# Routed attention and a hard-swish feed-forward block on one core: larger transposition groups, a new order in the prologue, and a fall-through at the close

## The chip, the cores and the metric

The kernel runs on one core of a Trainium2 chip. The metric is the device time of the whole launch in microseconds (us), taken as the median of several runs. The kernel before takes 1071.25 us (3 runs, 1070.79 to 1073.04). Beside the timed runs there is one profiled execution, whose first to last instruction span 1069.7 us.

## The reference, cut to what matters

Attention in which a query sees only the keys of its own cluster, then a feed-forward block. Batch 4, 8 heads, 768 positions, head dimension 64, 16 clusters; the block has 3072 tokens, width 512 and inner width 2048.

```python
q_assign = np.argmax(np.einsum('bhsd,hcd->bhsc', q_n, c_n), axis=-1)   # nearest centroid
k_assign = np.argmax(np.einsum('bhsd,hcd->bhsc', k_n, c_n), axis=-1)
mask = q_assign[:, :, :, None] == k_assign[:, :, None, :]
scores = scale * np.matmul(q, k.transpose(0, 1, 3, 2))
scores = np.where(mask, scores, -1000000000.0)
attn = softmax(scores)                      # with 1e-9 in the denominator
x = (attn @ v), heads side by side          # (4*768, 512)
h = x @ w_in
out = (h * np.clip(h + 3.0, 0.0, 6.0) / 6.0) @ w_out
```

The weights arrive as 64-bit floats and are decoded on the chip into 32-bit ones.

## The kernel before

Two heads are worked on together (a pair; there are 16), each with 768 positions as 6 chunks of 128. For each pair the queries and keys are transposed (`turn`), scored against the centroids (`cluster_scores`), turned into one-hot rows of the nearest cluster (`route`), and those rows are transposed (`route_turn`). For keys the one-hot rows are inverted and scaled by a large negative number, so that a second matmul into the same scores (`xm`) adds zero where the clusters agree and a large negative number elsewhere. Then come the exponential, the product with the values and a division.

A transposition on TensorE writes to PSUM, and ScalarE copies the result to SBUF. The transpositions and other small results share scratch banks of PSUM: two banks (`psum_m`) in the first half, one (`psum_t`) later.

```python
psum_t = pool("psum_t", 1, space=PSUM)
psum_m = pool("psum_m", 2, space=PSUM)

def scratch(shape, name):
    if st["early"]:
        return psum_m.tile(shape, F32, name=name, tag="m")
    return psum_t.tile(shape, F32, name=name, tag="t")

def turn(g, part):                     # four parts of NHC = 3 chunks
    ...
    pt = scratch([P, NHC, P], "pqk")
    for i in range(NHC):
        j = part * NHC + i
        nc.tensor.transpose(out=pt[:, i], in_=qk[:, j // NCH, j % NCH], identity=ident)
    dst = xf[:, part * NHC : (part + 1) * NHC]
    nc.scalar.copy(out=dst, in_=pt)
    ...

def route_turn(g, part):               # three parts of 4 chunks
    ...
    po = scratch([P, 4, P], "po")
    for i in range(4):
        j = part * 4 + i
        nc.tensor.matmul(
            po[:, i], lhsT=one_hot[:, j], rhs=(ident_q if j < NCH else ident_k),
            start=True, stop=True,
        )
    nc.scalar.copy(out=xm[:, part * 4 : part * 4 + 4], in_=po)
```

The preparation of the next pair is spread over the 12 steps of the current one. A step is two score blocks (`ps`), two products with the values (`pv`), a share of the feed-forward matmuls (`ph`, `X`, `Y`) and a share of the weight decoding on VectorE. At steps 2 and 8 the division falls due: `pd` is a matmul into a scratch bank, and VectorE takes its reciprocal (`rcp`) from there.

```python
def prep_items(g, r):
    if r in (0, 2):
        return [lambda: turn(g, r), lambda: turn(g, r + 1)]
    return {
        4: [lambda: cluster_scores(g)],
        6: [lambda: route(g)],
        8: [lambda: route_turn(g, 0), lambda: route_turn(g, 1)],
        10: [lambda: route_turn(g, 2)],
    }.get(r, [])
```

The prologue and the close:

```python
nc.scalar.dma_start(cen, centroids.rearrange("h c d -> (h c) d"))
load(0, "q", "k")
constants()                 # identities, ident_q and ident_k among them
load(0, "v")
load_weights(0)
centroid_norm()             # a chain of small VectorE steps, then a transposition (pc)
for part in range(4):
    turn(0, part)
load(1, "q", "k")
scores_qk(0)
scores_qk(1)
cluster_scores(0)           # pcs, copied to cs
route(0)                    # pr, then maximum and comparisons on VectorE
for part in range(3):
    route_turn(0, part)
...                         # the main sequence
# at the end: a flag ok tells whether the fast path's assumptions held for these inputs
with tc.If(tc.nc.values_load(ok[0:1, 0:1], min_val=0, max_val=1) == 0):
    general_path(inner, tc, *ins, out)      # not run for these inputs
```

Of the kernel before, what the change touches and what calls it, by code (L numbers as in the profile page):

```python
# [8 lines left out]
F32 = mybir.dt.float32  # L9
BF16 = mybir.dt.bfloat16  # L10
# [3 lines left out]
ACT = mybir.ActivationFunctionType  # L14
# [4 lines left out]
P = 128  # L19
NCH = S // P  # L20
NC2 = 2 * NCH
HALF = S // 2
NHC = NCH // 2
# [17 lines left out]
FAR = 2.0**60  # L41
# [75 lines left out]
def fast_path(ctx, tc, ok, q, k, v, centroids, moe_w_in, moe_w_out, out):  # L117
# [3 lines left out]
    nc = tc.nc  # L121
# [5 lines left out]
    const = pool("const", 1)  # L127
# [15 lines left out]
    psum_t = pool("psum_t", 1, space=PSUM)  # L143
    psum_m = pool("psum_m", 2, space=PSUM)
# [3 lines left out]
    g_sb = const.tile([P, 7, NFT // 2, P], F32, name="g_sb")  # L148
    ident = const.tile([P, P], F32, name="ident")
    ident_q = const.tile([P, P], BF16, name="ident_q")  # L150
    ident_k = const.tile([P, P], BF16, name="ident_k")
    ones = const.tile([P, D], F32, name="ones")
    half_c = const.tile([P, 1], F32, name="half_c")
    low_c = const.tile([P, 1], F32, name="low_c")
# [1 line left out]
    one_hot = const.tile([P, NC2, P], BF16, name="one_hot")  # L156
# [7 lines left out]
    st = {}  # L164
    later = []

    def scratch(shape, name):

        if st["early"]:
            return psum_m.tile(shape, F32, name=name, tag="m")  # L170
        return psum_t.tile(shape, F32, name=name, tag="t")

    def load(g, *names):
        if g >= NPAIR:
            return
        b, h = divmod(2 * g, H)
        for name in names:
            if name == "v":  # L180
                dst = st["v", g] = vp.tile([P, NCH, 2, D], F32, name="vt")
            elif name == "q":
                st["qk", g] = qkp.tile([P, 2, NCH, 2, D], F32, name="qk")
            if name != "v":
                dst = st["qk", g][:, "qk".index(name)]
            src = {"q": q, "k": k, "v": v}[name]
            for t in range(2):
                nc.sync.dma_start(dst[:, :, t], src[b, h + t].rearrange("(p j) d -> p j d", p=P))
# [66 lines left out]

    def constants():
        make_identity(nc, ident)
        nc.vector.tensor_copy(out=ident_q, in_=ident)
        nc.vector.tensor_scalar_mul(out=ident_k, in0=ident, scalar1=-FAR)
        for t in range(2):  # L260
            nc.vector.tensor_reduce(
                out=parity[:, t : t + 1],
                in_=ident.rearrange("p (h t c) -> p t h c", t=2, c=C)[:, t], axis=AX.XY, op=ALU.max,
            )
        nc.gpsimd.memset(half_c, 0.5)
        nc.gpsimd.memset(low_c, 1.0 / BOUND)
        nc.gpsimd.memset(ones, 1.0)
        nc.gpsimd.memset(w_low, W_LOW)
        nc.gpsimd.memset(one_hot, 0.0)

    def centroid_norm():
        cn = unit_rows(nc, smallp, cen, D)

        nc.scalar.activation(out=w_totals[:, 0, 0:1], in_=w_low, func=ACT.Exp)

        wide = smallp.tile([P, 2, D], F32, name="cenwide")
        for t in range(2):
            nc.vector.tensor_scalar_mul(out=wide[:, t], in0=cn, scalar1=parity[:, t : t + 1])
        pc = scratch([P, P], "pc")
        nc.tensor.transpose(out=pc, in_=wide, identity=ident)  # L280
        nc.vector.tensor_copy(out=cnT, in_=pc)


# [3 lines left out]
    def turn(g, part):  # L287
        if part == 0:
            st["xf", g] = xp.tile([P, NC2, P], F32, name="xf")
        qk, xf = st["qk", g], st["xf", g]  # L290
        pt = scratch([P, NHC, P], "pqk")
        for i in range(NHC):
            j = part * NHC + i
            nc.tensor.transpose(out=pt[:, i], in_=qk[:, j // NCH, j % NCH], identity=ident)  # L294
        dst = xf[:, part * NHC : (part + 1) * NHC]
        nc.scalar.copy(out=dst, in_=pt)  # L296
        if part == 3:
            st.pop(("qk", g))


# [2 lines left out]
    def cluster_scores(g):  # L303
        c0, xf = (2 * g) % H * C, st["xf", g]
        ps = scratch([P, 512], "pcs")[:, 0 : NC2 // 4 * P]
        for a in range(4):
            nc.tensor.matmul(  # L307
                ps[a * 2 * C : (a + 1) * 2 * C], lhsT=cnT[:, c0 : c0 + 2 * C], rhs=xf[:, a::4],
                start=True, stop=True,
            )  # L310
        cs = st["cs", g] = rtp.tile([P, NC2 // 4, P], F32, name="cs")
        nc.scalar.copy(out=cs, in_=ps)
# [30 lines left out]
    def route_turn(g, part):  # L343
        if part == 0:
            st["xm", g] = xp.tile([P, NC2, P], BF16, name="xm")
        xm = st["xm", g]
        po = scratch([P, 4, P], "po")
        for i in range(4):
            j = part * 4 + i
            nc.tensor.matmul(  # L350
                po[:, i], lhsT=one_hot[:, j], rhs=(ident_q if j < NCH else ident_k),
                start=True, stop=True,
            )
        nc.scalar.copy(out=xm[:, part * 4 : part * 4 + 4], in_=po)  # L354


    def where(n):
# [3 lines left out]
    def scores_qk(n):  # L361
        g, hf, j = where(n)
        st["ps", n] = psum_s.tile([P, 2, 512], F32, name="ps")
        scores_part(n, st["xf", g], True)
# [179 lines left out]
    def prep_items(g, r):  # L544

        if g >= NPAIR:
            return []
        if r in (0, 2):
            return [lambda: turn(g, r), lambda: turn(g, r + 1)]
        return {  # L550
            4: [lambda: cluster_scores(g)],
            6: [lambda: route(g)],
            8: [lambda: route_turn(g, 0), lambda: route_turn(g, 1)],
            10: [lambda: route_turn(g, 2)],
        }.get(r, [])

    per_pair = 2 * NCH
# [30 lines left out]
    with tc.manual_schedule():  # L588
        nc.scalar.dma_start(cen, centroids.rearrange("h c d -> (h c) d"))
        load(0, "q", "k")  # L590
        constants()
        load(0, "v")
        load_weights(0)
        centroid_norm()
        for part in range(4):
            turn(0, part)
        load(1, "q", "k")
        scores_qk(0)
        scores_qk(1)
        cluster_scores(0)  # L600
        route(0)
        for part in range(3):
            route_turn(0, part)

        for n in range(0, total + lag_d + 2, 2):
            g, r = divmod(n, per_pair)
            for i in (n, n + 1):
                if i < total:
                    scores(i)
            for i in (n - lag_v, n - lag_v + 1):  # L610
                if 0 <= i < total:
                    attn_v(i)
            m = n - lag_d + 1
            if m >= 0 and m % NCH == NCH - 1:
                later.append(divide(m))
            prep = prep_items(g + 1, r)
            if r == 4 and prep:
                prep.pop()()
            if n == DECODED:
                st["early"] = False  # L620
            if m >= 0 and m % per_batch == per_batch - 1:
                fill += ffn_items(m // per_batch)
            if r == 6:
                load(g + 2, "q", "k")
                load(g + 1, "v")
            want = items_by(n + 2) - done if n < total else len(fill)
            want = min(want, len(fill))
            done += want
            for i in range(max(len(prep), want)):
                if i < want:  # L630
                    fill.pop(0)()
                if i < len(prep):
                    prep[i]()
            for step in decode[: share[r]]:
                step()
            del decode[: share[r]]
            for check in checks:
                check()
            checks, later[:] = later[:], []

        for check in checks:
            check()
# [3 lines left out]
    good = smallp.tile([P, 2, NG], F32, name="good")  # L646
    fit = smallp.tile([P, 2, NW], F32, name="fit")
    alone = smallp.tile([P, 2, NPAIR], F32, name="alone")
    for got, sums, *bounds in (
        (good, totals, BOUND, 0.0), (fit, w_totals, W_HIGH, 0.0), (alone, counts, NC2, -NC2 * (C - 1.0)),  # L650
    ):
        for a, bound in enumerate(bounds):
            nc.vector.tensor_scalar(
                out=got[:, a], in0=sums[:, a], scalar1=bound, scalar2=None, op0=ALU.is_le
# [320 lines left out]
@with_exitstack  # L975
def kernel(
    ctx: ExitStack,
    tc: tile.TileContext,
    q: bass.AP,
    k: bass.AP,  # L980
    v: bass.AP,
    centroids: bass.AP,
    moe_w_in: bass.AP,
    moe_w_out: bass.AP,
    out: bass.AP,
):
    ins = (q, k, v, centroids, moe_w_in, moe_w_out)
    flagp = ctx.enter_context(tc.tile_pool(name="flagp", bufs=1))
    ok = flagp.tile([1, 1], I32, name="ok")
    with ExitStack() as inner:  # L990
        fast_path(inner, tc, ok, *ins, out)
    with tc.If(tc.nc.values_load(ok[0:1, 0:1], min_val=0, max_val=1) == 0):
        with ExitStack() as inner:
            general_path(inner, tc, *ins, out)

# [31 lines left out]
```

## Time and profile before

| what | before |
|---|---|
| time, median of 3 runs | 1071.25 us |
| span of the profiled execution | 1069.7 us |
| first transposition of queries (`pqk`) starts | 6.63 us |
| first masked scores (`ps<-xm`) start | 17.11 us |
| last matmul (`pl`) starts | 1062.03 us |
| one copy of 128x384 from `pqk` | 0.483 us, 64 of them |
| one copy of 128x512 from `po` | 0.584 us, 48 of them |
| one reciprocal of 128x384 | 2.553 us, 32 of them |

The names are those of the trace: PE is TensorE's matmuls, PEld its weight loads, DVE is VectorE, ACT ScalarE, POOL GpSimd, SP SyncE. L350 is line 350 of the kernel. A row of the form `out<-in` names the tile written and those read. Times at the left of a timeline are from the start of the span; a bracket at the end of a row tells how long the engine stood idle before it and what it waited for. Matmuls overlap, so the busy time of one (for example 381 ns) is longer than the distance between two.

### The profile page before, as it was taken

The page shows a single profiled execution, that of the slowest core. Times are in us where ns is not written, and L with a number is a line of the kernel's source. Part 1 is how long each engine was busy: PE and PEld are TensorE (multiplying, and loading weights), DVE is VectorE, ACT ScalarE, POOL GpSimd, SP SyncE. Part 2 cuts the span into 40 slices and gives each one's busy share as a digit, 9 for nine tenths or more (in the row PEclk, how much of TensorE's full clock was granted, in tenths as well). Part 3 has the DMA queues.
Part 4 walks back from the last instruction along what each step waited for, and adds up shares of the span by engine and source line. Part 5 has one row for each costly group of instructions (what it writes and reads, how often), then busy time and mean ns, then how long its engine had stood idle before and what let it go on. Part 6 is the DMA issues. An engine that isn't in the chain of part 4 may idle for free.

```text
span 1069.7 us, 13428 instructions
## 1 busy us (share of the span) xinstructions
PE 1033.1 (97%) x5490; PEld 723.1 (68%) x5490; DVE 460.4 (43%) x658; ACT 392.3 (37%) x796; POOL 305.5 (29%) x171
## 2 busy tenths in 40 slices
PE   6999999999999999999999999999999999999997
PEld 3444454546888866667676766767676688888886
DVE  5799987688241331521342333152135132314141
ACT  5888876674121232342332333233233120201010
POOL 2777755554100023232232223222323200000000
PEclk9999999999999999999999999999999999999999
DMA  5444544330000201101020020200000000000000
GB/s 144 114 123 124 143 124 103 84 104 1 20 1 9 56 1 44 20 1 45 21 45 1 20 45 1 64 1 15 21 1 1 14 6 21 0 20 1 20 1 24
DMA packets 83543, 42.94 MB, mean 40 GB/s; under 512 B 76304, under 2 KB 76304, under 8 KB 83472
## 3 DMA queue, kind: packets, MB, share of 16 engines
q1 hardware_dynamic: 83328, 41.95, 15.0%
q8 instruction: 45, 0.74, 0.3%
q14 instruction: 26, 0.21, 0.1%
q10 hardware_dynamic: 144, 0.03, 0.0%
HBM read 35.68 MB, written 6.29 MB: 39 GB/s over the span
## 4 chain that ended last, share of the span: by engine, by line
PE 89%; ACT 5%; DVE 4%; issue 1%; POOL 0%; ACTq 0%; DVEq 0%; POOLq 0%
PE ph L476 31%; PE Y L494 16%; PE ps L370 14%; PE X L494 11%; PE pv L399 11%; PE pqk L294 2%; DVE g_sb L488 2%; PE pd L420 2%; PE po L350 1%; PE pcs L307 1%; DVE rcp L424 1%; ACT ex L382 1%; ACT xm L354 1%; ACT wsize L214 1%; ACT xf L296 1%
## 5 line engine op out<-in xcount | busy, mean ns | idle before, releaser
L389 POOL TENSOR_TENSOR acc<-acc,ex 128x768 f32<-128x768 f32 x128 | 244.3, 1909 | 368.5 <-ACT ex L382 362.9
L476 PE MATMUL ph<-xT,w_in_sb 128*128 128x256 f32 x1536 | 343.8, 381 | 0.0
L476 PEld LDWEIGHTS ph<-xT,w_in_sb 128*128 128x128 f32 x1536 | 287.8, 190 | 56.3 <-issue 10.2
L443 ACT ACTIVATE g_sb<-ph,half_c 128x512 f32<-128x512 f32 x96 | 66.0, 687 | 316.0 <-PE ph L476 316.0
L444 DVE SCALAR_TENSOR_TENSOR g_sb<-g_sb,ph 128x512 f32<-128x512 f32 x96 | 66.0, 687 | 254.8 <-ACT g_sb L443 254.8
L382 ACT ACTIVATE ex<-ps 128x768 f32<-128x768 f32 x192 | 148.4, 804 | 66.1 <-PE ps L370 65.8
L370 PE MATMUL ps<-xf 64*128 64x384 f32 x768 | 167.5, 515 | 1.2 <-ACT ex L382 0.8
L399 PE MATMUL pv<-ex,vt 128*64 128x384 f32 x768 | 145.6, 500 | 0.0
L424 DVE RECIPROCAL rcp<-pd 128x384 f32<-128x384 f32 x32 | 81.7, 2553 | 62.9 <-PE pd L420 61.8
L386 POOL TENSOR_TENSOR acc<-ex 128x768 f32<-128x768 f32 x32 | 59.0, 1843 | 173.2 <-ACT ex L382 173.2
L488 DVE TENSOR_TENSOR g_sb<-g_sb 128x256 f32<-128x256 f32 x192 | 103.7, 581 | 3.3
L399 PEld LDWEIGHTS pv<-ex,vt 128*64 128x64 f32 x768 | 46.7, 136 | 80.9 <-issue 77.0
L370 PEld LDWEIGHTS ps<-xf 64*128 64x128 f32 x768 | 63.9, 188 | 46.7 <-issue 32.2
L501 DVE TENSOR_TENSOR y<-y,Y 128x256 f32<-128x256 f32 x48 | 20.2, 421 | 171.4 <-PE Y L494 170.7
L494 PE MATMUL Y<-w_out_sb,g_sb 128*128 128x256 f32 x384 | 88.0, 382 | 0.0
L494 PE MATMUL X<-w_out_sb,g_sb 128*128 128x256 f32 x384 | 87.7, 381 | 0.0
L494 PE MATMUL Y<-T,g_sb 128*128 128x256 f32 x384 | 87.0, 380 | 0.0
L494 PEld LDWEIGHTS Y<-w_out_sb,g_sb 128*128 128x128 f32 x384 | 72.0, 190 | 16.5 <-issue 7.2
L494 PEld LDWEIGHTS X<-w_out_sb,g_sb 128*128 128x128 f32 x384 | 72.1, 190 | 14.2 <-issue 3.0
L494 PEld LDWEIGHTS Y<-T,g_sb 128*128 128x128 f32 x384 | 72.1, 190 | 9.3
L370 PE MATMUL ps<-xm 64*128 64x384 bf16 x384 | 63.8, 327 | 0.0
L296 ACT COPY xf<-pqk 128x384 f32<-128x384 f32 x64 | 30.0, 483 | 53.3 <-PE pqk L294 53.3
(83 smaller groups left out, 642.3 us busy)
## 6 DMA issues: line engine op xcount, KB each, us to landing
raw<-in_moe_w_in_dram SPq DMA_DIRECT2D x16, 512.0 KB, 3.8
raw<-in_moe_w_out_dram SPq DMA_DIRECT2D x16, 512.0 KB, 3.6
qk<-in_q_dram SPq DMA_DIRECT2D x32, 192.0 KB, 4.2
qk<-in_k_dram SPq DMA_DIRECT2D x32, 192.0 KB, 4.4
vt<-in_v_dram SPq DMA_DIRECT2D x32, 192.0 KB, 4.2
out_dram<-y SPq DMA_DIRECT2D x24, 256.0 KB, 2.2
cen<-in_centroids_dram ACTq DMA_DIRECT2D x1, 32.0 KB, 1.8
```

What stands on the lines that cost most here:

```text
L296: nc.scalar.copy(out=dst, in_=pt)
L370: nc.tensor.matmul(st["ps", n][:, t, 0:HALF], lhsT=x[r, NCH + j], rhs=x[r, hf * NHC : (hf + 1) * NHC], start=first, stop=not first,)
L382: nc.scalar.activation(out=ex, in_=sc, func=ACT.Exp, scale=SM_SCALE)
L386: nc.gpsimd.tensor_tensor(out=acc, in0=st["ex", n - 1], in1=ex, op=ALU.add)
L389: nc.gpsimd.tensor_tensor(out=acc, in0=acc, in1=ex, op=ALU.add)
L399: nc.tensor.matmul(pv[t * D : (t + 1) * D], lhsT=vt[:, j, t], rhs=ex[:, t], start=(j == 0), stop=(j == NCH - 1),)
L424: nc.vector.reciprocal(out=rcp, in_=pd)
L443: nc.scalar.activation(out=g, in_=h, func=ACT.Relu, bias=half_c, scale=1.0 / 6.0)
L444: nc.vector.scalar_tensor_tensor(out=g, in0=g, scalar=1.0, in1=h, op0=ALU.min, op1=ALU.mult)
L476: nc.tensor.matmul(ph[:, t * HC : (t + 1) * HC], lhsT=w_in_sb[:, kt, f * P : (f + 1) * P], rhs=xT[:, kt, 2 * m * P : 2 * (m + 1) * P], sta ...
L488: nc.vector.tensor_tensor(out=out_, in0=in0, in1=in1, op=op)
L494: nc.tensor.matmul(bank[:, half * HC : (half + 1) * HC], lhsT=g_sb[:, kind, i], rhs=w[:, i], start=(first and i == 0), stop=(last and i == ...
```

## The change

It has three parts.

- **Larger groups.** `turn` works in three parts of 4 chunks, and `route_turn` in two parts of 6. So that 6 chunks fit in one bank, the one-hot rows are now transposed as bf16 into a bf16 tile, and not multiplied into a 32-bit one. The large negative factor of the keys, which was in a second identity `ident_k`, is applied by ScalarE as it copies.
- **The prologue.** 14 transpositions of the identity matrix are put ahead of the real ones, while TensorE has nothing to do; their result is not used. The queries and keys are transposed before the centroids. Cluster scores and routing come ahead of, or between, the first two score blocks. `ident_q` is made later on VectorE.
- **The close.** The branch over the general path is told which of its two sides should follow on without a jump.

The diff, cut to its core:

```diff
-    def scratch(shape, name):
+    def scratch(shape, name, dtype=F32):
...
     def constants():
         make_identity(nc, ident)
-        nc.vector.tensor_copy(out=ident_q, in_=ident)
-        nc.vector.tensor_scalar_mul(out=ident_k, in0=ident, scalar1=-FAR)
...
+        warm = psum_t.tile([P, 4, P], F32, name="warm", tag="t")
+        for i in range(14):
+            nc.tensor.transpose(out=warm[:, i % 4], in_=ident, identity=ident)
...
+    def centroid_turn():              # split off from centroid_norm
         pc = scratch([P, P], "pc")
-        nc.tensor.transpose(out=pc, in_=wide, identity=ident)
+        nc.tensor.transpose(out=pc, in_=st.pop("wide"), identity=ident)
         nc.vector.tensor_copy(out=cnT, in_=pc)
...
-        pt = scratch([P, NHC, P], "pqk")
-        for i in range(NHC):
-            j = part * NHC + i
+        pt = scratch([P, 4, P], "pqk")
+        for i in range(4):
+            j = part * 4 + i
...
-        po = scratch([P, 4, P], "po")
-        for i in range(4):
-            j = part * 4 + i
-            nc.tensor.matmul(
-                po[:, i], lhsT=one_hot[:, j], rhs=(ident_q if j < NCH else ident_k),
-                start=True, stop=True,
-            )
-        nc.scalar.copy(out=xm[:, part * 4 : part * 4 + 4], in_=po)
+        po = scratch([P, NCH, P], "po", BF16)
+        for i in range(NCH):
+            nc.tensor.transpose(out=po[:, i], in_=one_hot[:, part * NCH + i], identity=ident_q)
+        dst = xm[:, part * NCH : (part + 1) * NCH]
+        nc.scalar.activation(out=dst, in_=po, func=ACT.Copy, scale=-FAR if part else 1.0)
...
-        if r in (0, 2):
-            return [lambda: turn(g, r), lambda: turn(g, r + 1)]
         return {
+            0: [lambda: turn(g, 0), lambda: turn(g, 1)],
+            2: [lambda: turn(g, 2)],
             4: [lambda: cluster_scores(g)],
             6: [lambda: route(g)],
-            8: [lambda: route_turn(g, 0), lambda: route_turn(g, 1)],
-            10: [lambda: route_turn(g, 2)],
+            8: [lambda: route_turn(g, 0)],
+            10: [lambda: route_turn(g, 1)],
         }.get(r, [])
...
         centroid_norm()
-        for part in range(4):
+        for part in range(3):
             turn(0, part)
+        centroid_turn()
+        nc.vector.tensor_copy(out=ident_q, in_=ident)
         load(1, "q", "k")
+        cluster_scores(0)
         scores_qk(0)
+        route(0)
         scores_qk(1)
-        cluster_scores(0)
-        route(0)
-        for part in range(3):
+        for part in range(2):
             route_turn(0, part)
...
-    with tc.If(tc.nc.values_load(ok[0:1, 0:1], min_val=0, max_val=1) == 0):
+    good = tc.nc.values_load(ok[0:1, 0:1], min_val=0, max_val=1)
+    with tc.If(good == 0, preferred_fallthrough_block=False):
```

More of the change, by code (lines that the diff above doesn't have):

```diff
@@ L150, in fast_path @@
     ident_q = const.tile([P, P], BF16, name="ident_q")
-    ident_k = const.tile([P, P], BF16, name="ident_k")
     ones = const.tile([P, D], F32, name="ones")
@@ L165, in fast_path @@
     later = []
-    def scratch(shape, name):
+    def scratch(shape, name, dtype=F32):
         if st["early"]:
-            return psum_m.tile(shape, F32, name=name, tag="m")
-        return psum_t.tile(shape, F32, name=name, tag="t")
+            return psum_m.tile(shape, dtype, name=name, tag="m")
+        return psum_t.tile(shape, dtype, name=name, tag="t")
     def load(g, *names):
@@ L278, in centroid_norm @@
             nc.vector.tensor_scalar_mul(out=wide[:, t], in0=cn, scalar1=parity[:, t : t + 1])
+        st["wide"] = wide
+    def centroid_turn():
         pc = scratch([P, P], "pc")
-        nc.tensor.transpose(out=pc, in_=wide, identity=ident)
+        nc.tensor.transpose(out=pc, in_=st.pop("wide"), identity=ident)
         nc.vector.tensor_copy(out=cnT, in_=pc)
@@ L290, in turn @@
         qk, xf = st["qk", g], st["xf", g]
-        pt = scratch([P, NHC, P], "pqk")
-        for i in range(NHC):
-            j = part * NHC + i
+        pt = scratch([P, 4, P], "pqk")
+        for i in range(4):
+            j = part * 4 + i
             nc.tensor.transpose(out=pt[:, i], in_=qk[:, j // NCH, j % NCH], identity=ident)
-        dst = xf[:, part * NHC : (part + 1) * NHC]
+        dst = xf[:, part * 4 : part * 4 + 4]
         nc.scalar.copy(out=dst, in_=pt)
-        if part == 3:
+        if part == 2:
             st.pop(("qk", g))
```

## The prediction

> **What bounds the kernel now.** I read the engine summary first, then the slices, then TensorE's waits, and last the order of time around single waits.
>
> ```profile
> PE 1033.1 (97%) x5490; PEld 723.1 (68%) x5490; DVE 460.4 (43%) x658; ACT 392.3 (37%) x796; POOL 305.5 (29%) x171
> ...
> PE   6999999999999999999999999999999999999997
> ```
>
> TensorE (PE) is busy 97% of the span and only the first and last slices fall short. Its matmuls overlap, so busy alone is no proof, but their spacing is steady: the product rows show 16 records of 256 columns in 3.65 us, 216 ns apart, for long stretches. So TensorE's program is the path, and time can be won only where it stands still: at the start, at the end, and in the waits between. The list of TensorE's waits, from 18 us on, is short:
>
> ```profile
> PE po L350 <- ACT xm L354: 7.4, 10, 1.0
> PE pqk L294 <- ACT xf L296: 7.2, 11, 0.8
> PE po L350 <- DVE rcp L424: 4.9, 4, 1.2
> PE ps L370 <- ACT ex L382: 0.8, 3, 0.3
> ```
>
> The columns are total us, times, longest. Together 20.3 us: that is all the idle time of 1044 us. The timeline around one wait of the first kind shows what it is:
>
> ```profile
> 61.67 0.40 PE L350 MATMUL po<-ident_q,one_hot 128*128 128x128 bf16 x4
> ...
> 62.11 0.59 ACT L354 CAST xm<-po 128x512 bf16<-128x512 f32 x1 [1.54 <-PE po L350]
> 62.74 0.27 PE L350 MATMUL po<-ident_q,one_hot 128*128 128x128 bf16 x2 [0.67 <-ACT xm L354]
> ```
>
> Four one-hot chunks fill a PSUM bank, ScalarE (ACT) empties it in 0.59 us, and the next four chunks go into the same bank, so TensorE waits out the copy. In the built program of the kernel before, two `po` groups with nothing between them share a bank 10 times, and two `pqk` groups 11 times: exactly the counts of the first two waits.
>
> [...] the transpositions at 6.6 us are about 213 ns apart, those at 22.6 us about 120 ns, and the granted clock is 0.91 from 6 to 18 us. [...]
>
> **Part 1: larger groups.** Per pair of heads, queries and keys are turned in 3 groups of 4 chunks and not 4 of 3, and the one-hot rows in 2 groups of 6 and not 3 of 4. TensorE's own work stays: 12 chunks each. A copy of 384 columns takes 479 ns and one of 512 584 ns, so 0.82 ns a column; one of 768 should take 584 + 256 x 0.82 = 794 ns. ACT has 3 x 584 + 2 x 794 for 4 x 479 + 3 x 584, 0.33 us less per pair; it is not the bound.
>
> What counts is which groups follow each other in one bank. In the built program of the changed kernel no two `po` groups do (each has a step of its own), and two `pqk` groups do 4 times: twice before 260 us, where such a wait was 0.82, and twice later, where it was 0.57. With 0.10 more for the longer copy: 2 x 0.92 + 2 x 0.67 = 3.2. So 7.4 + 7.2 - 3.2 = **11.4 us** leave the path. The four waits of 1.2 us for the reciprocal stay: there `po` waits for a bank that VectorE (DVE) still reads, because four subtractions of the gate stand before the reciprocal in DVE's queue.
>
> At 386 us such a wait (1.24) and a `po` wait (0.67) fall within 2 us, and the matmuls after it run slow (the next three `ps` groups take 1.07, 0.54 and 1.50 us where 0.92, 0.33 and 0.81 are usual): one half-clock window of 3.4 us, so 1.7 lost. With only 1.24 idle I give it an even chance not to happen: **0.9 us**.
>
> **Part 2: the prologue.** The first scores are completed by the masks (`ps<-xm`) at 17.11 us, and this is where the main sequence begins. Before, the centroid chain on DVE held the transpositions until 6.63. After, they come first. Their data decides then: the keys land 4.0 us after the second issue at 2.8, so at 6.9; 14 warming transpositions at 0.21 take from 1.3 to 4.4 and are out of the way by then. The queries, issued by 1.5 and 3.7 us on the way, are there by 5.2. Six query chunks fill 5.2 to 6.5; the six key chunks run from 7.0 to 8.3, and the third copy ends at 9.05. Then cluster scores without the two score blocks before them:
>
> - Warm: `pcs` 0.86 to 10.0, copy to 10.55, `pr` behind one score block at 10.7, 0.55, reduction and two comparisons (0.56 + 0.62 and gaps) to 12.5, one-hot groups to 13.0, two copies of 0.79 to 14.25. `ps<-xm` at 14.3: 2.8 gained, and 0.7 more as the next six transpositions (1.54 us before, 0.88 when warm) run warm.
> - Cold: `pcs` 1.7, the score block and `pr` twice as long: `ps<-xm` at 16.25, 0.9 gained.
>
> Between 3.5 and 0.9, I take the middle: **2.2 us**. The next pair's loads move from 9.6 to about 8.3 with it, so they hold nothing up.
>
> **Part 3: the close.** After the flag is read each engine branches over the general path:
>
> ```profile
> L992 SPq EVENT_SEMAPHORE  x8: 17/17/17, 1067.8 to 1068.3; - x8
> ...
> L992 PEldq COMPARE_BRANCH  x1: 4444/4444/4444, 1064.2 to 1064.2; - x1
> ...
> L992 PEldq EVENT_SEMAPHORE  x1: 51/51/51, 1068.7 to 1068.7; - x1
> ```
>
> The branch costs TensorE 4.4 us and SyncE (SP) 3.1. The change makes the empty alternative the fall-through. But in the built program the blocks stand as: empty alternative, general path (7881 instructions), end. The alternative ends in a jump to the end, over the same general path. [...] TensorE would arrive at 1068.7 as before; SP does its eight waits first and jumps about 1.3 us later, which could cost up to 1. [...] I take **0.3 us** gained.
>
> Sum: 11.4 + 0.9 + 2.2 + 0.3 = 14.8, and 1071.25 - 14.8 = **1056.4 us**.
>
> **The rivals.**
>
> *DVE takes over in the first stage.* The table of stages has it:
>
> ```profile
> 60.00:140.00 80.00, 75.30 (x493) 33.28 (x491) 74.88 (x86) 67.27 (x154) 57.90 (x31) 1.00 0.46 125
> ```
>
> Third comes DVE: 74.88 of 80 us, with the decoding of the weights. The waits to be removed there are 5.2 us before 142 us, 0.6 per half pair, so DVE would be at 98%. If its queue falls behind, one-hot rows and reciprocals come late and TensorE waits for them. Against it: TensorE waits for no DVE result there now, and the one-hot rows stand ready 1.3 to 3.0 us before use, enough for the lag that could build up. If it holds all the same: about 1061.
>
> *The bf16 transposition is slower than the matmul it replaces.* At twice the 55 ns spacing of the `po` matmuls, 192 x 55 ns = 10.5 us: 1067. Against: an fp32 product of 256 columns leaves two records of 216 ns, 1.69 ns a column, an fp32 transposition 0.85, a bf16 matmul 0.43; transposing is not the slower form in fp32.
>
> *Everything pays.* Warm from the start, the far jump gone (3 us) and the reciprocal waits shortened too (up to 4.9): 1047 to 1050. Nothing in the program moves the reciprocals.
>
> *The waits were slack for others.* If ACT or DMA was just keeping up, the removed idle time returns as waits on `ex`. ACT is at 84% in the stage from 60 to 140 and its work shrinks; weight loads wait for DVE, not the other way. I give this 1 to 2 us within the range.
>
> **Range and chances.** Solid are the 11.4 (counted waits, counted banks), less perhaps 2 for the DVE rival. Prologue 0 to 4, close -1 to +3, clock window -1.7 to +1.7 by where it falls. That gives **1050.5 to 1062**. Faster by over 2% is below 1049.8, which needs nearly every open term at its best: 0.12. Slower by over 2% needs something that nothing here points to: 0.01. Within 2%: 0.87.
>
> **What would show it.** In the profile after, TensorE's waits for the copies of `po` should be gone after 18 us and those of `pqk` be about 4, the waits for the reciprocal still 4 of 1.2. `po` groups should stay about 55 ns apart, and the copy of 768 columns take about 0.79 us. `ps<-xm` should first come between 14.3 and 16.3 us; their spacing tells whether the warming transpositions raised the clock. At the close, the gap from the last output's issue to the end shows whether a jump still costs about 4 us on TensorE. I am wrong if new waits on one-hot rows or DVE appear between 60 and 260 us, if the reciprocal waits change, or if the far jump is gone.

## The result, and the profile after

The changed kernel takes 1057.18 us (median of 4 runs, 1056.73 to 1057.35) against 1071.29 us for the kernel before, measured beside it. The ratio is 0.9865, with a 95% interval of 0.9848 to 0.9882: 14.1 us less. The predicted time was 1056.4.

The engine summary of the page of the changed kernel, first line of its first part:

```profile
PE 1029.7 (98%) x5504; PEld 722.0 (68%) x5504; DVE 471.1 (45%) x657; ACT 388.0 (37%) x764; POOL 303.5 (29%) x171
```

TensorE is still the bound, with 14 matmuls more (the idle transpositions) in a span of 1055.5 us and not 1069.7. Cut at the first masked scores and at the last matmul, the span shows where the 14.2 us came from:

| stage | before, us | after, us | difference |
|---|---|---|---|
| start to the first masked scores | 17.11 | 14.35 | -2.76 |
| from there to the last matmul (`pl`) | 1044.92 | 1033.20 | -11.72 |
| last matmul to the end | 7.67 | 8.00 | +0.33 |

For the middle stage, here are TensorE's waits in the changed kernel from 16 us on (columns: total us, times, longest):

```profile
PE po L353 <- DVE rcp L425: 5.0, 4, 1.2
PE ps L371 <- ACT ex L383: 3.2, 6, 1.1
PE pqk L298 <- ACT xf L300: 3.0, 4, 0.8
PE ps L371 <- ACT xm L355: 1.6, 5, 0.5
PE po L353 <- DVE one_hot L331: 0.6, 1, 0.6
```

The ten waits of `po` for its copy are gone, and those of `pqk` are 4 and not 11, as the banks of the built program had said. The four for the reciprocal are untouched. New are 12 short waits of 5.4 us in all, for exponentials, masks and one-hot rows; before there were 3 with 0.8.

The prologue, in order of time on TensorE (start, time from first to last, group):

```profile
1.36 3.25 PE L270 MATMUL warm<-ident 128*128 128x128 f32 x14 [1.36 <-POOL ident masks.py:199]
4.84 1.41 PE L298 MATMUL pqk<-ident,qk 128*128 128x128 f32 x6 [0.23 <-DMA qk<-in_q_dram]
7.05 0.85 PE L298 MATMUL pqk<-ident,qk 128*128 128x128 f32 x6 [0.79 <-DMA qk<-in_k_dram]
...
14.35 0.50 PE L371 MATMUL ps<-xm 64*128 64x384 bf16 x4 [1.27 <-ACT xm L355]
```

Fourteen transpositions in 3.25 us are 0.21 us apart, half clock; six in 0.85 us are 0.11 apart, full clock. The rise came between, before any matmul other than a transposition. The measure for this comes from the kernel before: six transpositions take 1.54 us at 17.86, where its clock column says 0.50, and 0.88 at 22.59, where it says 1.00.

The close, one line of the source with all its instructions (columns: engine, instruction, times, ns min/median/max, first and last start):

```profile
L996 SPq EVENT_SEMAPHORE  x8: 17/17/17, 1050.9 to 1051.4; - x8
...
L996 PEldq COMPARE_BRANCH  x2: 83/2028/3973, 1049.7 to 1050.0; - x2
```

There are two branches where there was one: the first falls through in 83 ns, and the second takes 3973 ns, against 4444 for the only one before.

### The profile page after: what moved, and what is told of

It reads as the page before. It is cut to its first block, busy times and chain, and to the rows that moved or that the text cites. A ratio compares the mean times of both kernels' runs of the same rounds, so it can differ in the third digit from the quotient of the medians.

```text
span 1055.5 us, 13430 instructions
## 1 busy us (share of the span) xinstructions
PE 1029.7 (98%) x5504; PEld 722.0 (68%) x5504; DVE 471.1 (45%) x657; ACT 388.0 (37%) x764; POOL 303.5 (29%) x171
## 4 chain that ended last, share of the span: by engine, by line
PE 88%; DVE 6%; ACT 4%; issue 1%; DMA 1%; SPq 0%; DVEq 0%; ACTq 0%
PE ph L477 31%; PE Y L495 16%; PE ps L371 13%; PE X L495 11%; PE pv L400 10%; PE pqk L298 2%; DVE g_sb L489 2%; PE pd L421 2%; DVE rcp L425 1%; ACT ex L383 1%; PE pcs L311 1%; ACT xm L355 1%; PE po L353 1%; ACT wsize L213 1%; DVE wunit L239 1%
## 5 line engine op out<-in xcount | busy, mean ns | idle before, releaser
L489 DVE TENSOR_TENSOR g_sb<-g_sb 128x256 f32<-128x256 f32 x192 | 113.5, 632 | 3.2
L495 PEld LDWEIGHTS X<-w_out_sb,g_sb 128*128 128x128 f32 x384 | 72.1, 190 | 14.2 <-issue 3.6
L495 PE MATMUL X<-T,g_sb 128*128 128x256 f32 x192 | 44.0, 382 | 0.0
```

Source lines behind the costliest of these rows:

```text
L489: nc.vector.tensor_tensor(out=out_, in0=in0, in1=in1, op=op)
L495: nc.tensor.matmul(bank[:, half * HC : (half + 1) * HC], lhsT=g_sb[:, kind, i], rhs=w[:, i], start=(first and i == 0), stop=(last and i == ...
```

## The experiments

Each was timed beside the kernel before; ratios have their 95% intervals. The first three do one part of the change alone.

### The larger groups alone

The `turn`, `route_turn`, `scratch` and `prep_items` edits on the prologue order and the close of before.

```diff
+        centroid_turn()               # ahead of the transpositions, as before
         for part in range(3):
             turn(0, part)
...
-        for i in range(14):           # no idle transpositions
```

> Only the larger groups, on the prologue and the close of before. Theory A (the gain is the waits of two groups that follow each other in one PSUM bank): the waits of po for the copy go from 10 to 0 and those of pqk from 11 to 4, new waits on ACT cost about 5, so 11 us less than before: about 1060. Theory B (the main part of the 14 us comes from the prologue and from a clock that no longer falls back): 5 to 7 us less, about 1065.

Measured: 1060.79 us, ratio 0.9897 (0.9882 to 0.9913), so about 11 us less. Theory A had 1060, theory B 1065. The waits in its profile are those of the changed kernel, to within 1.5 us: none of `po` for its copy, 4 of `pqk`.

### The prologue alone

```diff
+        for i in range(14):
+            nc.tensor.transpose(out=warm[:, i % 4], in_=ident, identity=ident)
...
         for part in range(4):
             turn(0, part)
+        centroid_turn()
+        cluster_scores(0)
         scores_qk(0)
+        route(0)
         scores_qk(1)
```

> Only the new order of the prologue and the 14 idle transpositions, on the groups of 3 and 4 and the close of before. Both theories of the profile: the first masked scores move from 17.1 us to about 14.4, and the two transposition groups after them run at full clock, so 3 to 4 us less than before: about 1067.5. If the groups and the prologue are independent, this gain and that of the larger groups add up to the whole.

Measured: 1068.5 us, ratio 0.9969 (0.9955 to 0.9984), 3.3 us less. The profile taken of it does not show the 14.4 us that was expected: its masked scores come at 15.35 us. The key chunks run at full clock (0.84 us at 7.17), but then the clock falls back, and the cluster scores take 1.51 us at 9.06, where the changed kernel has 0.85. At 1070.38 us the profiled execution is the slowest of the six. The three ratios multiply to 0.9897 x 0.9969 x 0.9997 (the next experiment) = 0.9863, and the whole change has 0.9865: within the noise the parts add up.

### The close alone

```diff
-    with tc.If(tc.nc.values_load(ok[0:1, 0:1], min_val=0, max_val=1) == 0):
+    good = tc.nc.values_load(ok[0:1, 0:1], min_val=0, max_val=1)
+    with tc.If(good == 0, preferred_fallthrough_block=False):
```

> Only the fall-through at the close. If the far jump only moves, the time from the last matmul to the end goes from 7.7 to about 8.0 us: 0.3 us more than before, within the noise. If the fall-through pays by itself, up to 3 us less.

Measured: 1071.33 us, ratio 0.9997 (0.9989 to 1.0006). No gain; in its profile the time from the last matmul to the end is 8.1 us. The fall-through moves the far jump and does not remove it (in the changed kernel its second branch takes TensorE the 3973 ns).

### The change without the idle transpositions

```diff
-        for i in range(14):
-            nc.tensor.transpose(out=warm[:, i % 4], in_=ident, identity=ident)
```

> The changed kernel without the 14 idle transpositions. If they raise the clock (theory W): the later transpositions of the prologue run 213 ns apart, the first masked scores come at 15.5 to 16.3 and not 14.35, and the time is 1.5 to 2.5 us above that of the changed kernel, about 1059. [...]

Measured: 1059.55 us, ratio 0.9884 (0.9869 to 0.9899). That is 2.0 us above the changed kernel by the ratios, though the two intervals overlap. The profile is clearer. Its prologue in order of time:

```profile
7.12 1.51 PE L295 MATMUL pqk<-ident,qk 128*128 128x128 f32 x6 [0.62 <-DMA qk<-in_k_dram]
...
9.41 1.51 PE L308 MATMUL pcs<-xf,cnT 128*32 128x384 f32 x8 [0.48 <-DVE ident_q L596]
...
16.89 0.50 PE L368 MATMUL ps<-xm 64*128 64x384 bf16 x4 [1.27 <-ACT xm L352]
```

The key chunks take 1.51 us and the cluster scores 1.51, where the changed kernel has 0.85 and 0.85, and the masked scores come 2.5 us later, at 16.89, after the 15.5 to 16.3 that were expected. In this pair of profiles the idle transpositions raise the clock.

### Old group sizes, but no two in a row

The kernel before with its groups of 3 and 4; only their place in the step changes.

```diff
+            prep = prep_items(g + 1, r)
+            if len(prep) > 1:
+                prep.pop(0)()
             for i in (n - lag_v, n - lag_v + 1):
                 if 0 <= i < total:
                     attn_v(i)
...
-            prep = prep_items(g + 1, r)
```

> The kernel before with its groups of 3 and 4 chunks, its prologue and its close; only the first of two groups of a step is issued between the scores and the products with the values, so that no two groups follow each other in one bank. Theory A (succession in a bank is what costs): the 21 waits of po and pqk for their copies go, at 0.85 us each, and 8 to 14 us are gained, about 1060, as with the larger groups. Theory S (fewer and larger groups pay, through fewer copies on ACT): no gain, about 1071.

Measured: 1064.09 us, ratio 0.9934 (0.9918 to 0.9951): 7.1 us gained with not one group larger. So most of the groups' 11 us is succession in a bank, not size. It is less than that 11, and less than the 8 to 14 of theory A. One reason is that waits took the place of waits:

```profile
PE po L350 <- DVE one_hot L327: 4.7, 5, 2.1
PE po L350 <- DVE rcp L424: 3.6, 4, 0.9
PE pqk L294 <- ACT xf L296: 2.7, 3, 1.4
PE pqk L294 <- DVE rcp L424: 1.5, 2, 0.8
```

The first group of a step is now issued before the products with the values, so it asks for its one-hot rows earlier than VectorE delivers them. But with 0.8 us for exponentials the waits of this run come to 13.3 us, and those of the changed kernel to 13.4, so they do not set the two apart. The other reason is the new place itself:

```profile
59.07 0.33 PE L370 MATMUL ps<-xm 64*128 64x384 bf16 x2
59.33 0.40 PE L350 MATMUL po<-ident_q,one_hot 128*128 128x128 bf16 x4
59.66 1.51 PE L399 MATMUL pv<-ex,vt 128*64 128x384 f32 x8
```

From the masked scores to the values it is 0.59 us here and 0.26 in the kernel before (59.33 to 59.59), so four `po` matmuls, 55 ns apart, cost 0.33 and not 0.22. At about 0.1 us each, the 45 groups that were moved (three in each of 15 pairs) cost some 4.5 us; this is an estimate. The longest wait was also followed by a stretch at half clock, in which eight `pv` matmuls take 2.12 us and not 1.51:

```profile
87.26 0.40 PE L350 MATMUL po<-ident_q,one_hot 128*128 128x128 bf16 x4 [2.11 <-DVE one_hot L327]
87.58 2.12 PE L399 MATMUL pv<-ex,vt 128*64 128x384 f32 x8
```

Two groups per pair fit into two late steps with nothing to share; three don't. That, as I read it, is what the larger size buys.

### Larger groups, again in a row

```diff
-            8: [lambda: route_turn(g, 0)],
-            10: [lambda: route_turn(g, 1)],
+            8: [lambda: route_turn(g, 0), lambda: route_turn(g, 1)],
```

> The changed kernel with both one-hot groups of 6 in one step, one after the other in one bank. Theory A: ten waits of about 0.8 + 0.2 us come back with the groups as large as in the change, so 6 to 10 us more than the changed kernel: 1063 to 1067. Theory S: no change, 1057.

Measured: 1064.85 us, ratio 0.9941 (0.9924 to 0.9958), 8.1 us above the changed kernel by the ratios. Its waits have the ten back:

```profile
PE po L353 <- ACT xm L355: 9.5, 10, 1.1
```

And its order of time shows a second cost where two waits stand close together:

```profile
378.31 0.49 PE L353 MATMUL po<-ident_q,one_hot 128*128 128x128 bf16 x6 [1.24 <-DVE rcp L425]
379.71 0.80 PE L353 MATMUL po<-ident_q,one_hot 128*128 128x128 bf16 x6 [0.90 <-ACT xm L355]
380.44 1.65 PE L371 MATMUL ps<-xf 64*128 64x384 f32 x4
```

Four `ps` matmuls take 1.65 us and not 0.92: TensorE runs at half clock, and does so to 383 us.

### Raw weights one chunk further ahead

```diff
-    rawp = decoding.enter_context(tc.tile_pool(name="rawp", bufs=2))
+    rawp = decoding.enter_context(tc.tile_pool(name="rawp", bufs=3))
...
-            load_weights(i + 1)
+            load_weights(i + 2)
...
         load_weights(0)
+        load_weights(1)
```

> The changed kernel with a third buffer for the raw weights, loaded one chunk further ahead. Theory C (VectorE is late with the decoding, so the raw loads are late, the totals on ACT wait for them, the exponentials behind them come late and TensorE waits for a score bank): the waits of ps for ex (3.2 us in all) fall under 1 us and 2 to 4 us are gained: about 1054. Rival D (VectorE's work itself is the bound to about 142 us): the waits move to the one-hot rows and reciprocals, and under 1 us is gained.

Measured: 1056.41 us, ratio 0.987 (0.9854 to 0.9886), not to be told from the changed kernel: the 2 to 4 us of theory C did not come. The waits of `ps` for `ex` fell from 3.2 to 1.7 us, as theory C had it, but not below 1, and ScalarE waits for no raw load any more. The waits for one-hot rows and reciprocals did not grow (0.6 and 5.0 us), as rival D had it. So late raw loads account for about half of these waits; what holds the other half was not found.

### The combining steps after the reciprocal

```diff
+                    def combine():
                         for out_, in0, in1, op in (
                             ...
                         ):
                             nc.vector.tensor_tensor(out=out_, in0=in0, in1=in1, op=op)
+                    owed.append(combine)
...
                 if i < want:
+                    while owed:
+                        owed.pop()()
                     fill.pop(0)()
```

> The changed kernel with the four combining steps of the gate put off to the next feed-forward item, so that the reciprocal stands ahead of them in VectorE's queue. If the four waits of 1.2 us of po for the reciprocal come from that queue: they go, and 5 to 6 us are gained, about 1051.5. If the reciprocal itself is too slow for one feed-forward item (3.46 us) to cover: they stay.

The combining steps are four additions and subtractions on VectorE, `g_sb<-g_sb` in the trace.

Measured: 1051.88 us, ratio 0.9821 (0.9804 to 0.9837), 4.7 us below the changed kernel by the ratios. All its waits from 16 us on:

```profile
PE ps L372 <- ACT ex L384: 3.1, 6, 1.0
PE pqk L299 <- ACT xf L301: 3.0, 4, 0.8
PE ps L372 <- ACT xm L356: 2.7, 5, 1.3
PE po L354 <- DVE one_hot L332: 0.6, 1, 0.6
```

The reciprocal is gone from the list: the queue was the cause, not the reciprocal's 2.55 us. (Of the 2.7 us for `xm`, 1.27 belong to the prologue, which ends later here.) This run also shows that idle transpositions don't always raise the clock in time. Its prologue in order of time:

```profile
1.36 3.25 PE L271 MATMUL warm<-ident 128*128 128x128 f32 x14 [1.36 <-POOL ident masks.py:199]
...
6.75 1.51 PE L299 MATMUL pqk<-ident,qk 128*128 128x128 f32 x6 [0.30 <-DMA qk<-in_k_dram]
...
16.19 0.50 PE L372 MATMUL ps<-xm 64*128 64x384 bf16 x4 [1.27 <-ACT xm L356]
```

The same 14 transpositions, and the key chunks still run at half clock. In the six other profiles with idle transpositions the key chunks take 0.84 or 0.85 us.

### What the experiments point to, together

The change with the close of before, the combining steps put off, the raw weights ahead, and the first `pqk` group of a pair issued between scores and values (for step 0 alone, so that the one-hot rows are not asked for early).

```diff
+            prep = prep_items(g + 1, r)
+            if r == 0 and prep:
+                prep.pop(0)()
             for i in (n - lag_v, n - lag_v + 1):
```

> The changed kernel with the close of before, the combining steps of the gate put off, the raw weights one chunk further ahead, and the first transposition group of a pair issued between scores and values, so that no copy is waited for in one bank at all. If the waits are independent: the reciprocal waits (5.0 + 4 x 0.17) and the pqk waits (3.0 + 4 x 0.17) go, 0.8 for the raw loads, 0.3 for the close: 10 us below the changed kernel, about 1047. If the waits take each other's place as with the spaced groups (one-hot rows or exponentials late): 1050 to 1052.

Measured: 1049.07 us, ratio 0.9794 (0.9781 to 0.9808): faster than both kernels, 22 us below the kernel before. Its waits from 16 us on:

```profile
PE ps L372 <- ACT ex L384: 1.5, 5, 0.4
PE ps L372 <- ACT xm L356: 1.4, 4, 0.5
PE po L354 <- DVE one_hot L332: 0.6, 1, 0.6
```

Only 3.5 us of waits are left of the 20.3 before. The time is 2 us above the 1047 expected. In its profile a stretch at half clock follows the first masked scores (eight transpositions take 2.12 us at 15.12), after a wait of 0.41 us for the next pair's queries. The second raw chunk loads ahead of them; that this is why they are late was not tried by itself. The stretch is not the whole of the 2 us: the next kernel has none in its profile and takes as long. By the 0.1 us for a moved group, the 15 groups moved here cost about 1.5 us, an estimate that the 1047 did not have.

### A fuller warm-up

The same with 17 idle transpositions, and 6 more in the wait for the keys.

```diff
-        for i in range(14):
+        for i in range(17):
...
+            if j == NCH and "warm" in st:
+                warm = st.pop("warm")
+                for w in range(6):
+                    nc.tensor.transpose(out=warm[:, w % 4], in_=ident, identity=ident)
```

> The same with 17 idle transpositions at the start and 6 more in the wait for the keys, so that TensorE has no idle stretch up to the last key chunk. [...] the first masked scores at 14.2 to 14.6, and 0 to 2 us less than without, 1 on average. If the six more only stand in the way of the keys: 0.5 us more.

Measured: 1048.85 us, ratio 0.9799 (0.9783 to 0.9815): no difference that can be told. In its profile the keys were not held up (they run at 6.99) and the masked scores come at 14.29. Whether it makes the clock rise in every execution is left open; one profile can't show it.

## Why the prediction was right, point by point

**What bounds the kernel** held. TensorE's waits were the only idle time, and removing them moved the end.

**Larger groups, 11.4 us.** The step that counted banks held to the count: 10 waits to 0, 11 to 4, the rest of the `pqk` waits 3.0 us where 3.2 was predicted. The part measured alone gives 11, with the clock term in it. But two terms were mis-sized and cancelled.

- A wait costs more than its idle time. Idle is counted from the modelled end of the last matmul, while in a stream the next one starts earlier. In the timeline shown in the prediction, four `po` matmuls start at 61.67; at 55 ns apart the fifth is due at 61.89 and starts at 62.74: 0.85 lost, where the bracket says 0.67. If the 17 waits removed are all like this one, it is 17 x 0.18, about 3 us more gained than I counted: an estimate from one wait.
- New waits came, 4.6 us more of them than before. The rival that I put at 1 to 2 us was right in kind and larger than I gave it, and my argument against it ("weight loads wait for DVE, not the other way") failed at its second half. VectorE is at 76.02 of 80 us in the stage from 60 to 140, as its row in the table of stages shows:

```profile
60.00:140.00 80.00, 76.19 (x495) 35.31 (x495) 76.02 (x85) 64.96 (x144) 57.52 (x30) 1.00 0.49 128
```

It frees the raw buffers late, the loads start late (from 16 to 142 us their issues wait 86.9 us for VectorE's `wunit`, in the kernel before 87.3), and ScalarE's totals wait for them with the exponentials queued behind: at 119.73 us the totals start after a wait of 1.26 for a raw load, at 121.26 the exponentials, and at 122.10 TensorE after a wait of 0.96 for them. The list of ScalarE's waits up to 142 us has these first two lines, 4.4 us, where the kernel before had the third, 0.7:

```profile
ACT wsize L213 <- DMA raw<-in_moe_w_out_dram: 2.3, 3, 1.3
ACT wsize L213 <- DMA raw<-in_moe_w_in_dram: 2.1, 2, 1.7
ACT wsize L214 <- DMA raw<-in_moe_w_in_dram: 0.7, 1, 0.7
```

So the chain runs VectorE, DMA, ScalarE, TensorE. The run with the raw weights ahead confirms it for half of the waits. The prediction's own sign of being wrong, a new wait on one-hot rows between 60 and 260 us, came once: 0.60 us at 107.94. The larger part of the rival, 1061 us with VectorE as the bound, did not come.

**The clock, 0.9 us.** It was mis-sized for this profile. Of the half-clock stretch in the kernel before (clock 0.50 for 3.41 us, from 387.9 to 391.3), these are the wait ahead of it and one of the slow groups (0.81 us is usual):

```profile
386.99 0.27 PE L350 MATMUL po<-ident_q,one_hot 128*128 128x128 bf16 x2 [0.67 <-ACT xm L354]
388.47 1.50 PE L370 MATMUL ps<-xf 64*128 64x384 f32 x4
```

It did go (1.7, half of the 3.41), and so did one at 15.9 to 19.3 (also 3.41), after the old prologue, about 1.1 of it behind the first masked scores. In other profiles of kernels that keep the pair of neighbouring waits, half-clock stretches stand near 380 us, near 645 us or at both (clock 0.94 over 370 to 400 or 630 to 660 us, which fits 3.4 us of the 30 at half clock); where one of the two waits is gone, there is none at these places (clock 1.00 in the changed kernel, the groups alone and the change without idle transpositions). Together the middle stage has 11.6 (idle removed) + 3 + 2.8 (clock) - 4.6 = 12.8; measured were 11.72. The 1.1 left over would be the surcharge of the new waits, which I didn't measure one by one.

**The prologue, 2.2 us, between cold (16.25) and warm (14.3).** Both times were hit: 14.35 in the changed kernel, 16.19 in the run whose clock rose late. The keys ran at 7.05 where 7.0 was predicted. What the profile of before hid is that its own 17.11 was late: the three other profiled kernels with the old prologue reach this point between 15.7 and 15.9. The clock rose late in it: the eight `ps` matmuls at 9.52 take 2.93 us, and 1.56 to 1.77 in the three others. The changed prologue gains about 1.5 over those. In all four profiles of the old one a half-clock stretch of 3.4 us follows between 15.9 and 20.1 us (clock 0.76 over 13 to 20 us in three of them, 0.57 over 16 to 20 in the run of the close alone; 1.7 lost), and of the eight with the new order only one has it after its masked scores (a second, the prologue alone, has one ahead of them). The two gains come to 3.2, an estimate beside the 3.3 measured for the prologue alone. The 2.2 was the middle between two cases, so being near the measured gain says little for the path to it.

**The warm-up.** For fp32 transpositions the measurement is this: after 14 of them and six more the spacing went from 0.21 to 0.11 us, with no other matmul before, and without the idle ones it stayed at 0.21 (the six key chunks in 1.51 us). In three other runs (larger groups in a row, raw weights ahead, and all together) the queries already take 0.85 us, from 5.06 to 5.22 on, after the 14 alone. The old prologue in the run of the close alone points the same way, as its `ps` matmuls follow 13 transpositions and nothing else and run at full clock (eight in 1.56 us at 9.51). But the same 14 raised the clock before the keys in one run (six in 0.85 us) and not in another (1.51); what decides between the two was not shown.

**The close, 0.3 us gained.** The size was small as predicted and the sign was wrong in the profiles: from the last matmul to the end it is 7.62 to 7.79 us in the six with the old close and 7.88 to 8.13 in the six with the new one. The timed runs (0.9989 to 1.0006) can't tell 0.3 us. The far jump moved (4444 ns at one branch before, 3973 at the second after), as the block order said; what makes it take 4 us was not shown. SyncE ran its eight waits first and jumped 3.9 us after the last matmul (1051.5), where it had branched after 2.6: 1.3 us later, as expected. The gap to the end grew only by 0.33, within the "up to 1".

**The bf16 transposition** costs what the matmul did: 12 in 0.84 us, (0.84 - 0.22) / 11 = 56 ns apart. That rival is out. The copy of 768 columns takes 0.811 us where 0.794 was worked out.

**The sum.** In the runs of single parts, groups and clock gave 11.0 us where 11.4 + 0.9 = 12.3 were predicted, and the prologue 3.3 where 2.2 were. These misses cancel, so that the total came within 0.8 us is in part luck; the counted waits, which carry most of it, are not.

## What to carry to other kernels

Where TensorE, the bounding engine here, wrote two groups one after the other into one scratch bank, it waited out the copy, 0.7 us each (14.6 us in 21 waits); the built program's bank numbers counted these waits (10 and 11 before, 0 and 4 after). Moving one group past other work removes them too, but look at what the new place costs: about 0.1 us a group in the run with the old sizes. Before taking a wait off, look at the engine behind it that is nearly full and follow what it feeds, through loads and queues, since the next wait may come by that road. VectorE's queue ran in order here (in the kernel before the reciprocal stood behind 4.79 us of combining steps at 378.6 us): in such a queue, put the result that another engine waits for ahead of those that nobody waits for yet. Here that was worth 4.7 us.

## What the hardware showed that I had not expected

- **Two neighbouring waits can cost more than their sum.** 1.24 us and 0.7 to 0.9 us of idle time within 2 us were followed by half clock for 3.4 us, 1.7 us lost, at six of eight such places in four profiles. Half clock also followed one wait of 2.11 us (eight `pv` matmuls in 2.12 us). A wait of 1.24 alone was not followed by it in these profiles (clock 1.00 over 370 to 400 and 630 to 660 us in the changed kernel).
- **The clock column starts late.** In the run without idle transpositions it says 1.00 from 8 to 12 us, while the cluster scores at 9.41 take 1.51 us and not 0.85. So the 0.91 that the prediction reads from 6 to 18 us in the kernel before is the stretch from 15.9 us on, not the slow start. Go by the spacing of equal matmuls.
- **VectorE's combining steps took longer beside GpSimd.** Four combining steps of 128x256 take 1.55 us where GpSimd is idle (the run with the steps put off, at 374.8 us) and 4.79 us beside its additions (the kernel before, at 378.6 us).
